# Moving rows of five transfers between DMA engines: K loads and dk stores cut into two transfers by rows

## The chip, the cores and the metric

The kernel runs on one core of one Trainium2 chip. The time is the device time of that core in microseconds (us), median of several executions. A core has 16 DMA engines, which carry every load and every store.

## The reference, cut to what matters

```python
B, H, Sq, Sk, D = 2, 32, 1, 8192, 128          # bf16
scores = einsum("bhqd,bhkd->bhqk", q, k) * D ** -0.5
out    = einsum("bhqk,bhkd->bhqd", softmax(scores), v)
# returned: out and the gradients dq, dk, dv for a given grad_out
```

There are 64 heads with one query row each. For every head 2 MB of K and 2 MB of V are read and 2 MB each of dk and dv are written, 537 MB in all. Nothing is read or written twice.

## The kernel before

K and V of a head are loaded as tiles of 128 rows (SBUF partitions) by 16 KB. There are 12 such tiles. dk and dv are computed in place of K and V and stored from the same tile, so a load has to wait until the store of the tile that it replaces has landed.

```python
load_eng = nc.sync          # SP: descriptors made by hardware
store_eng = nc.gpsimd       # POOL: descriptors made by software
...
def load(i, w, pieces=(NCH,)):                      # w: 0 for K, 1 for V
    t = kvp.tile([P, NT, D], BF16, tag=f"kv{slot_of(i, w)}", name="kvt")
    src = (v_v if w else k_v)[i]
    c = 0
    for m in pieces:
        n0, n1 = c * CH, (c + m) * CH
        pin(load_eng.dma_start(out=t[:, n0:n1, :], in_=src[:, n0:n1, :]))
        c += m
...
def outer(i, w, c, ends):                           # dk or dv, in place, then its store
    ...
    pin(store_eng.dma_start(out=dst[:, b0:b1, :], in_=h.tile[w][:, b0:b1, :]))
```

Of the kernel before, what the change touches and what calls it, by code (L numbers as in the profile page):

```python
# [16 lines left out]
CW = 64  # L17
NG = 2
NTILE = 12

@with_exitstack
def kernel(
# [12 lines left out]
    B, H, Sq, D = q.shape  # L36
# [5 lines left out]
    NT = Sk // P  # L42
# [5 lines left out]
    load_eng = nc.sync  # L48
    store_eng = nc.gpsimd
    pin = tc.keep_in_program_order  # L50
# [25 lines left out]
    def slot_of(i, w):  # L76

        n = 2 * i + w
        return n if n < NTILE else slot_of(i - NTILE // 2, 1 - w)

    def load(i, w, pieces=(NCH,)):
        h = heads[i]
        t = kvp.tile([P, NT, D], BF16, tag=f"kv{slot_of(i, w)}", name="kvt")
        h.tile[w] = t
        src = (v_v if w else k_v)[i]
        c = 0
        for m in pieces:
            n0, n1 = c * CH, (c + m) * CH
            pin(load_eng.dma_start(out=t[:, n0:n1, :], in_=src[:, n0:n1, :]))  # L89
            c += m  # L90

    load(0, 0, (1, 1, 2))

    qd_nat = evp.tile([P, CH, P], BF16, tag="ev", name="qd_nat")
    for w, a in enumerate((q, grad_out)):
        pin(load_eng.dma_start(out=qd_nat[:BH, w, :], in_=a.rearrange("b h s d -> (b h s) d")))  # L96

    load(0, 1)
    for j in range(1, min(NTILE // 2, BH)):
        load(j, 0)  # L100
        load(j, 1)
# [268 lines left out]
    def outer(i, w, c, ends):  # L370

        h = heads[i]
        n0 = c * CH
        shape = [P, CH, D // 2, 2]
        pin(
            nc.vector.tensor_tensor(  # L376
                out=h.tile[w][:, n0 : n0 + CH, :].rearrange("p n (e t) -> p n e t", t=2),
                in0=h.qb[w][:]
                .rearrange("p (e t) -> p e t", t=2)
                .unsqueeze(1)  # L380
                .to_broadcast(shape),
                in1=h.pair[w][:, n0 : n0 + CH, :].unsqueeze(2).to_broadcast(shape),
                op=ALU.mult,
            )
        )
        if c + 1 in ends:
            at = ends.index(c + 1)
            b0, b1 = (ends[at - 1] if at else 0) * CH, (c + 1) * CH
            dst = (dv_v if w else dk_v)[i]
            pin(store_eng.dma_start(out=dst[:, b0:b1, :], in_=h.tile[w][:, b0:b1, :]))  # L390

    A1 = NCH + 4
# [4 lines left out]
    last = list(range(1, NCH + 1))  # L397
    AHEAD = NTILE // 2

    prev = None  # L400
    for g in range(SL * BH + O0 + NCH + 4 - SL):
# [15 lines left out]
        if x := within(O1):  # L417
            outer(x[0], 1, x[1], last if x[0] == BH - 1 else whole)
        if x := within(O0):
            outer(x[0], 0, x[1], last if x[0] == BH - 1 else whole)  # L420
        ev = None
        if g < SL * BH:
            i, r = divmod(g, SL)
# [74 lines left out]
```

## Time and profile before

| | before |
|---|---|
| time, median of 2 runs | 1305.32 us (1304.26 to 1306.38) |
| busy: PE, DVE, ACT, POOL | 89%, 72%, 75%, 6% |
| HBM traffic over the span | 412 GB/s |
| packets of 16 KB, usual duration | 611 ns |

The prediction shows the DMA rows of the page, the load queue's waits, the end of the chain and five windows. One more part of the page is of use later, the DMA issues (out<-in, queue, operation, count, KB each, median us from issue to landing of the last share):

```profile
out_dram<-kvt POOLq DMA_DIRECT2D x126, 2048.0 KB, 40.4
kvt<-in_v_dram SPq DMA_DIRECT2D x64, 2048.0 KB, 49.3
kvt<-in_k_dram SPq DMA_DIRECT2D x63, 2048.0 KB, 49.4
```

A share is 8 packets of 611 ns. That a transfer needs eight to ten times as long is queueing: several stores and loads stand before it on the engine that finishes last.

### The profile page before, as it was taken

The numbers are of one execution on the slowest core, as the hardware profiler recorded it, in microseconds if no ns is written. First come the engines' busy times: TensorE is split into PE (matmuls) and PEld (weight loads), VectorE is DVE, ScalarE is ACT, GpSimd is POOL, SyncE is SP. The second block draws the span as 40 slices with busy tenths as digits, with TensorE's granted clock in tenths as the row PEclk, the third lists the DMA queues.
The fourth block names the chain that finished last, engine by engine and source line by source line (L and its number), as shares of the span: only waits on it lengthen the run. The fifth ranks groups of instructions, "written<-read, shape, count | busy, mean of one in ns | idle before, by whom it ended". The sixth has DMA issues, their size and how long they took to land.

```text
span 1303.1 us, 42566 instructions
## 1 busy us (share of the span) xinstructions
PE 1154.0 (89%) x19268; PEld 873.0 (67%) x19268; DVE 937.5 (72%) x2122; ACT 974.8 (75%) x641; POOL 72.4 (6%) x142
## 2 busy tenths in 40 slices
PE   6999998889898888988989888989898898888984
PEld 5777776667676666666766666667676676666662
DVE  2888887677776777767777677676776767777776
ACT  6888887777787777777778777777777777777771
POOL 0000000000000000000000000000000000000001
PEclk9999999899898999989989999898898989999986
DMA  9999999999999999999999999999999999999965
GB/s 390 423 427 427 427 427 427 428 426 430 427 427 427 427 427 429 427 428 427 429 427 427 429 427 424 418 420 425 421 416 420 419 421 421 418 421 422 394 281 206
DMA packets 38517, 539.67 MB, mean 414 GB/s; under 512 B 4544, under 2 KB 4544, under 8 KB 5824
## 3 DMA queue, kind: packets, MB, share of 16 engines
q1 hardware_dynamic: 19040, 268.51, 48.9%
q0 software_dynamic: 19296, 268.44, 48.7%
q8 instruction: 150, 2.46, 0.7%
q14 instruction: 31, 0.25, 0.0%
HBM read 268.47 MB, written 268.47 MB: 412 GB/s over the span
## 4 chain that ended last, share of the span: by engine, by line
issue 80%; DMA 11%; POOL 4%; DVE 2%; PE 1%; POOLq 0%; SPq 0%; DVEq 0%
DMA kvt<-in_v_dram 8%; POOL out_dram L390 4%; DMA out_dram<-kvt 3%; DVE kvt L376 1%; PE tp L166 1%; POOLq L390 0%; PE acc L321 0%; DVE sel L344 0%; PE dpw L177 0%; SPq L89 0%; SPq L96 0%; DVE sel L338 0%; PE sw L177 0%; PE acc L358 0%; DVE pair L252 0%
## 5 line engine op out<-in xcount | busy, mean ns | idle before, releaser
L168 ACT COPY ev<-tp 128x2048 bf16<-128x2048 bf16 x512 | 954.0, 1865 | 300.3 <-PE tp L166 290.6
L166 PE MATMUL tp<-ident_bf,kvt 128*128 128x128 bf16 x8192 | 573.4, 226 | 108.9 <-DMA kvt<-in_v_dram 91.1
L376 DVE TENSOR_TENSOR kvt<-qb,pair 128x2048 bf16<-128x2048 bf16 x512 | 621.1, 1214 | 0.2
L166 PEld LDWEIGHTS <-kvt 128*128 128x128 bf16 x8192 | 501.4, 102 | 116.2 <-DMA kvt<-in_v_dram 95.8
L177 PEld LDWEIGHTS <-ev 128*128 128x128 bf16 x8192 | 242.8, 96 | 211.2 <-issue 164.4
L321 PE MATMUL acc<-kvt,dS_pad 128*64 128x512 bf16 x1024 | 177.2, 430 | 1.3 <-DVE dqT L361 1.3
L321 PE MATMUL acc<-kvt,E_pad 128*64 128x512 bf16 x1024 | 159.8, 392 | 0.0
L177 PE MATMUL dpw<-qdT,ev 128*128 128x1 bf16 x4096 | 140.9, 164 | 12.0 <-DVE qb L159 10.7
L189 DVE TENSOR_REDUCE mp<-sw 128x1 f32<-128x64 f32 x64 | 14.3, 224 | 186.5 <-PE sw L177 186.5
L344 DVE SCALAR_TENSOR_TENSOR sel<-acc,diag,sel 128x128 f32<-128x128 f32 x384 | 134.6, 351 | 13.6
L177 PE MATMUL sw<-qdT,ev 128*128 128x1 bf16 x4096 | 142.5, 164 | 1.1 <-ACT ev L168 1.1
L390 POOL DMA_DIRECT2D out_dram<-kvt x134 | 71.3, 532 | 1219.2 <-DVE kvt L376 1186.8
L321 PEld LDWEIGHTS <-dS_pad 128*64 128x64 bf16 x1024 | 38.5, 113 | 26.9 <-issue 9.4
L229 DVE CAST E_pad<-E_f 128x64 bf16<-128x64 f32 x64 | 12.5, 195 | 60.6 <-ACT E_f L220 60.6
L321 PEld LDWEIGHTS <-E_pad 128*64 128x64 bf16 x1024 | 36.3, 108 | 21.0 <-issue 0.2
L358 PE MATMUL acc<-ones,sel 128*128 128x1 f32 x256 | 43.3, 239 | 6.2 <-DVE sel L344 6.2
L264 PE MATMUL dpw<-ld,ones 128*128 128x1 f32 x256 | 46.3, 250 | 0.1
L338 DVE TENSOR_SCALAR sel<-acc,diag 128x128 f32<-128x128 f32 x128 | 44.0, 344 | 0.0
L358 PEld LDWEIGHTS acc<-ones,sel 128*128 128x128 f32 x256 | 39.0, 193 | 7.3 <-DVE sel L344 7.3
L235 DVE CUSTOM_DVE_ANT_0 junk<-E_f,dpw 128x64 bf16<-128x64 f32 x64 | 14.1, 220 | 40.2 <-PE dpw L177 40.2
L159 DVE CAST qb<-dpw 128x128 bf16<-128x128 f32 x128 | 35.4, 277 | 6.0 <-PE dpw L150 6.0
L264 PEld LDWEIGHTS dpw<-ld,ones 128*128 128x128 f32 x256 | 38.2, 188 | 0.5 <-DVE ld L235 0.5
(42 smaller groups left out, 303.2 us busy)
## 6 DMA issues: line engine op xcount, KB each, us to landing
out_dram<-kvt POOLq DMA_DIRECT2D x126, 2048.0 KB, 40.4
kvt<-in_v_dram SPq DMA_DIRECT2D x64, 2048.0 KB, 49.3
kvt<-in_k_dram SPq DMA_DIRECT2D x63, 2048.0 KB, 49.4
out_dram<-kvt POOLq DMA_DIRECT2D x8, 512.0 KB, 11.3
kvt<-in_k_dram SPq DMA_DIRECT2D x2, 512.0 KB, 4.5
kvt<-in_k_dram SPq DMA_DIRECT2D x1, 1024.0 KB, 7.1
out_dram<-nat SPq DMA_DIRECT2D x2, 16.0 KB, 5.0
qd_nat<-in_q_dram SPq DMA_DIRECT2D x1, 16.0 KB, 6.8
```

The costliest lines, as they stand in the source:

```text
L159: pin(nc.vector.tensor_copy(out=h.qb[w][:], in_=h.qbp))
L166: pin(nc.tensor.transpose(tp[:, t, :], src[:, c * CH + t, :], ident_bf[:]))
L168: pin(nc.scalar.copy(out=ev[:], in_=tp[:]))
L177: nc.tensor.matmul(dst[:, c * CH + t : c * CH + t + 1], lhsT=ev[:, t, :], rhs=qdT[:, w, i : i + 1], start=True, stop=True,)
L189: pin(nc.vector.reduce_max(out=h.mp[:], in_=h.s, axis=AX.X))
L264: nc.tensor.matmul(out, lhsT=ones[:].to_broadcast([P, P]), rhs=col, start=True, stop=True)
L321: nc.tensor.matmul(h.acc[w][g : g + CW, :], lhsT=wts[:, n0 : n0 + CW], rhs=rows[:, n0 : n0 + QT, :].rearrange("p n d -> p (n d)"), start=( ...
L338: nc.vector.tensor_scalar(out=h.sel[:], in0=block, scalar1=diag[:, 0:1], scalar2=None, op0=ALU.mult)
L344: nc.vector.scalar_tensor_tensor(out=h.sel[:], in0=block, scalar=diag[:, b : b + 1], in1=h.sel[:], op0=ALU.mult, op1=ALU.add,)
L358: nc.tensor.matmul(h.acc[w][:, 0:1], lhsT=h.sel[:], rhs=ones[:], start=True, stop=True)
L376: nc.vector.tensor_tensor(out=h.tile[w][:, n0 : n0 + CH, :].rearrange("p n (e t) -> p n e t", t=2), in0=h.qb[w][:] .rearrange("p (e t) -> ...
L390: pin(store_eng.dma_start(out=dst[:, b0:b1, :], in_=h.tile[w][:, b0:b1, :]))
```

## The change

The intent is to even out the load of the DMA engines. Transfers of a row count that 16 doesn't divide use fewer engines, so three K loads and two dk stores are each cut into two transfers by rows, such that four to seven engines take most of the 2 MB and the others get relief.

```diff
+HEADS_IN = {10: (119, 9), 16: (102, 26), 22: (76, 52)}
+HEADS_OUT = {26: (119, 9), 32: (9, 119)}
...
+    def by_rows(eng, dst, src, rows):
+        p = 0
+        for m in rows:
+            pin(
+                eng.dma_start(out=dst[p : p + m], in_=src[p : p + m], max_dma_last_dim=NT * D)
+            )
+            p += m
...
+        if w == 0 and i in HEADS_IN:
+            by_rows(load_eng, t, src, HEADS_IN[i])
+            return
...
+            if w == 0 and i in HEADS_OUT:
+                pin(store_eng.inc_swdge_sem([], [], mode="reset_dge_cursor"))
+                by_rows(store_eng, dst, h.tile[w], HEADS_OUT[i])
+                return
```

The `max_dma_last_dim` makes two packets of 8 KB out of each row of 16 KB. The reset puts the cursor of the stores, the engine at which the next store that doesn't take all 16 begins, back to engine 0 (the prediction has the rule).

## The prediction

> **What bounds the kernel now.** The page first: no compute engine is near its limit (PE 89% busy, of modelled ends; DVE 72%, ACT 75%), while the DMA row is full for 38 of the 40 slices and the rate flat.
>
> ```profile
> DMA  9999999999999999999999999999999999999965
> GB/s 390 423 427 427 427 427 427 428 426 430 427 427 427 427 427 429 427 428 427 429 427 427 429 427 424 418 420 425 421 416 420 419 421 421 418 421 422 394 281 206
> q1 hardware_dynamic: 19040, 268.51, 48.9%
> q0 software_dynamic: 19296, 268.44, 48.7%
> q8 instruction: 150, 2.46, 0.7%
> ```
>
> The last line is the fetching of instructions, a third user of the same 16 engines. The rate is 427 in the first half and near 420 from slice 25 on: something gets worse. Next, who waits for whom on the load queue, and the chain of waits near the end:
>
> ```profile
> SPq L89 <- DMA out_dram<-kvt: 1140.6, 116, 24.2
> ...
> 1154.90 49.14 DMA kvt<-in_v_dram
> ...
> 1215.54 49.35 DMA kvt<-in_v_dram
> 1264.90 0.05 issue
> 1264.94 1.49 PE tp L166 x16
> ```
>
> Almost every load is issued only when a store has landed and freed its tile; a load then needs 49 us to land. A transfer puts 8 rows of 16 KB on each engine, and a packet of that size took 611 ns, so 8 rows beside 8 of a store (the queues alternate) are about 9.8 us of work. The other 40 us are queue, but not on all engines. The trace holds the 16 completion times of each transfer, one for each DMA engine, without the engine's number. Sorted, for the last V load (issued at 1215.5 us): seven from 1225.2 to 1226.4, eight from 1238.9 to 1243.0, one at 1264.9. So there are seven fast engines, eight middle ones, and one straggler, 22 us behind all others. The lag grows: behind the first engine the straggler was 4.4 us late for the load issued at 9.6 us, 12.5 at 252.5, 21.8 at 496.1, 27.4 at 617.5. Then it stays near 39 to 40, because the fast engines have caught up with the issue (10 to 12 us from issue to landing there, their own work and nothing else) and cannot get further ahead: that is the fall from 427 to 421. The windows (columns: busy time with count of PE, PEld, DVE, ACT, POOL; clock; DMA share; GB/s) show both this and the drain:
>
> ```profile
> 100.00:700.00 600.00, 544.18 (x9110) 412.01 (x9109) 442.42 (x997) 460.80 (x303) 32.41 (x61) 0.95 1.01 428
> 750.00:1200.00 450.00, 399.94 (x6688) 302.54 (x6686) 325.32 (x738) 338.06 (x223) 23.39 (x44) 0.95 1.01 421
> ...
> 1226.00:1243.00 17.00, 16.80 (x288) 12.40 (x285) 13.37 (x33) 14.22 (x10) 0.53 (x1) 0.95 0.86 363
> 1243.00:1265.00 22.00, 18.66 (x306) 14.05 (x303) 15.79 (x35) 16.23 (x11) 1.44 (x3) 0.92 0.54 226
> 1265.00:1292.00 27.00, 19.30 (x209) 11.81 (x209) 21.66 (x45) 7.77 (x6) 4.77 (x10) 0.70 0.72 289
> ```
>
> From 1226 us engines run dry while the straggler still owes loads. The end is its end too: the last quarter store is issued at 1291.6, 15 engines finish it by 1295.1, the straggler at 1301.1. **The straggler bounds the kernel from the first stores to the last byte.** Its pace: loads are issued 101.1 us per ten late in the run (1023.4 to 1124.5), 10.11 us for 16 of its packets, 0.632 us each; a fast one has 0.607 (the next packet starts some 4 ns before the 611 are over).
>
> **What the Trainium skill says.** *DMA: Bandwidth & Descriptors*, section "Why a DMA increments its semaphore by 16 and not by 1": the number of engines k is the largest up to 16 that divides the slowest dimension of both sides; loads from SP use the lowest-numbered k engines, stores from GpSimd k consecutive ones from a round-robin cursor, though some such direct copies take 16 engines all the same. Before, every transfer has a row count divisible by 16 and 16 completions, which agrees; smaller k does not occur. The same page, "Latency and other measured facts": engines 7 and 15 are usually slower than the rest. One straggler is seen here, its number is not. *Runtime: NRT & Kernel Launch*, "Instruction fetch mechanics": instructions come in blocks of 16 KiB over DMA; the 150 packets on q8 agree, and their durations repeat roughly every eight packets, which fits eight engines doing the fetching: the middle group.
>
> **The change part by part.** No arithmetic moves; on GpSimd, two cursor resets and two more stores are added, on SP three more loads. All that counts is rows per engine. With the skill's rule, 119 = 7 x 17 goes to 7 engines, 9 to 9, 102 = 6 x 17 to 6, 76 = 4 x 19 to 4, 26 and 52 to 13. Rows per engine, against 8 in an even transfer:
>
> ```
> engines       0-3   4-5    6    7-8   9-12  13-15
> K load 10      18    18   18      1     0      0
> K load 16      19    19    2      2     2      0
> K load 22      23     4    4      4     4      0
> dk store 26    17    17   17      1     1      1
> dk store 32     1     1    1      1    17     17
> sum            78    59   42      9    24     18
> less 5 x 8    +38   +19   +2    -31   -16    -22
> ```
>
> The store splits, which start from cursor 0, relieve exactly 7 and 8 of the two row sets; the loads relieve all above 6. This is a design against a straggler numbered 7, eight middle engines 8 to 15, and fast ones 0 to 6: 7 + 8 + 1, as the completion times have it. That the numbers belong to the groups so is my choice; the trace does not show it, and the skill's engine 7 supports it.
>
> Natural arrival at the last V load, if no engine had to wait: straggler 1264.9 and middle about 1241 as measured; fast: the lag of 4.1 us per 100 us (27.4 us at 667 us, where the load issued at 617.5 lands last) gives 52 at 1265, so 1213. Add rows:
>
> Engines 0 to 3: 1213 + 38 x 0.607 = 1236. Engines 4 and 5: 1213 + 19 x 0.607 = 1225. Engine 6: 1214. Engine 7: 1264.9 - 31 x 0.632 = 1245.3. Engine 8: 1241 - 19 = 1222. Engines 9 to 12: 1241 - 10 = 1231. Engines 13 to 15: 1241 - 13 = 1228.
>
> Engine 7 remains last, by 9 us. So the gain is 31 x 0.632 = 19.6 us, no more: the moved load comes out of an engine's work that is on the path everywhere, and lands on engines that had 52 us to spare. The tail shifts with it: after the last V load the straggler has stores until 1301.1, 36.2 us, and the compute up to the last store 26.7 us plus 3.5 to land; both stay. 1305.3 - 19.6 = 1285.7.
>
> Costs: K tiles 10, 16 and 22 land later. Engines 0 to 3 get 15 extra rows in the worst load, 18 us with stores between. All three put 36 rows (22 us) more on them and 17 (11 us) less on engine 7; at 400 us their natural lead is 16, so they are then about 17 us behind it. A load's slack is the 39 us of queue, so nothing should run dry. The pieces of 8 KB cost 0.306 against 0.3035 for half a large packet (such packets took 309 ns, 3 ns of overlap), under 0.2 us in all. A GpSimd reset falls in an engine 6% busy.
>
> **The rivals.** (1) The stores take 16 engines, the skill's exception: then only the loads relieve engine 7, 17 rows, 10.7 us: 1294.6. For it: no store of before shows k below 16; against: the odd row counts and the resets only make sense if k follows. (2) The straggler is 15 and the middle group 0 to 7. Then engine 15 gains 22 rows, 13.9 us, but engines 0 to 3 go from 1241 to 1264: the end barely moves, 1300 to 1308. For it: the skill names 15 as well; against: the author's choice of rows, which would be senseless. (3) Port conflicts: *DMA: Bandwidth & Descriptors*, "The descriptor swizzle", has each engine write one SBUF port in a 128-partition transfer; 17 or 19 rows on one engine cross several, so several engines may meet at one port. Only the row transfers are concerned, and ports average half load each way since loads and stores are equal; estimated at a few us on engines 0 to 6, within their margin of 9: 1286 to 1291. (4) A reset or the wider skew makes GpSimd or the loads wait for an emptied queue, up to a transfer's 40 us each: 1295 to 1330. Nothing in the profile speaks for it. (5) Over 2% faster would need 1279.2, 26 us; engine 7 loses only 19.6.
>
> **Range and chances.** I give the sum 75%, rivals 1 and 3 together 15, 2 and 4 five each. The predicted time is 1286 us, range 1281 to 1300; faster by over 2% 0.05, within 2% 0.92, slower by over 2% 0.03.
>
> **What would show it.** Right: the straggler's last V load completes near 1245, the slowest of the others about 9 us before, not 22; the drain from full DMA to the last load shrinks from 39 to about 30 us; the rate stays near 427 in slices 25 to 36; small row transfers show few completions late and the rest at once. Stores 26 and 32 in which one engine's share is 17 rows decide rival 1; K load 22 landing past its queue of 49 us by more than 20 speaks for 3. Wrong: a straggler of the same 22 us (then it is not engine 7 or 8), or new idle in the DMA row near 110 to 400 or 560 to 700 us (rival 4).

## The result, and the profile after

| | before | after |
|---|---|---|
| time, median of 2 runs | 1305.32 us | 1324.78 us (1324.24 to 1325.33) |
| ratio | | 1.0149, 95% interval 1.0105 to 1.0193 |
| HBM traffic over the span | 412 GB/s | 406 GB/s |

A ratio is the mean time of one kernel's fast runs over that of the other's of the same rounds, so it is not quite the ratio of the medians in the table. The change is 19.5 us slower; a gain of 19.6 us was predicted, and the range ended at 1300. That it stayed within 2%, which the prediction had given 0.92, is luck: the sign was wrong. All its outputs were correct.

The DMA part of the page of the changed kernel:

```profile
DMA  9999999999999999999999999999999999999973
GB/s 390 424 427 426 427 412 427 428 420 375 398 396 408 421 408 417 425 420 373 422 417 414 423 425 427 426 429 423 426 425 423 424 425 423 420 425 423 421 312 135
q1 hardware_dynamic: 19428, 268.51, 48.6%
q0 software_dynamic: 20224, 268.45, 48.4%
q8 instruction: 150, 2.46, 0.7%
```

The rate, flat at 427 in this part of the run before, has holes now: slice 6 (412), slices 10 to 16 (375 to 421) and slice 19 (373). A slice is 33 us, and K loads 10, 16 and 22 are issued at 130, 250 and 389 us, the cut stores at 573 and 678 us. And the last slice is at 135 GB/s where it was 206.

The windows of the changed kernel (columns as in the prediction) show what was going on in the holes and at the end:

```profile
170.00:210.00 40.00, 16.03 (x262) 11.96 (x259) 12.24 (x28) 13.11 (x10) 1.07 (x2) 0.70 1.01 416
...
290.00:330.00 40.00, 26.77 (x446) 20.09 (x444) 21.92 (x50) 23.01 (x16) 1.60 (x3) 0.88 1.01 383
330.00:470.00 140.00, 110.06 (x1862) 83.95 (x1862) 89.64 (x205) 93.68 (x62) 6.39 (x12) 0.87 0.99 407
```

```profile
1243.00:1271.00 28.00, 24.64 (x412) 18.47 (x409) 21.83 (x49) 21.60 (x14) 1.64 (x4) 0.94 0.94 395
1271.00:1300.00 29.00, 18.28 (x210) 11.59 (x210) 22.30 (x48) 7.77 (x6) 3.53 (x7) 0.76 0.65 265
1300.00:1323.40 23.40, 0.00 (x0) 0.00 (x0) 0.00 (x0) 0.00 (x0) 1.60 (x3) 0.50 0.22 88
```

Between 170 and 210 us the PE worked 16 of 40 us (35.7 before): it stood waiting for K tile 10, of which the seven engines delivered their shares only 63 to 71 us after the issue. The DMA share is still 1.01, because loads were queued on every engine. Between 290 and 330 us the DMA share is again 1.01, but with only 383 GB/s: the packets took longer. In the last 23 us no compute engine does anything; one engine empties its queue. The completion times of the last store of the changed kernel, after its issue at 1311.8 us: 15 of them at 2.7 to 2.9 us, one at 9.3. It was worse for the quarter store issued at 1297.0: 15 at 2.8 to 2.9 us, one at 20.4. So there is still one straggler, and its end has moved from 1301.1 to 1321.1 us. In the loads it hardly shows any more: the last V load landed at 1271.1 us on its last engine and at 1266.6 on the one before (1264.9 and 1243.0 in the kernel before).

Who waited for whom on the store queue of the changed kernel (us in total, times, longest), and the issues, show a side effect:

```profile
POOL out_dram L407 <- DVE kvt L389: 1089.4, 116, 32.4
POOL out_dram L407 <- DMA out_dram<-kvt: 61.8, 9, 12.9
```

```profile
out_dram<-kvt POOLq DMA_DIRECT2D x124, 2048.0 KB, 56.8
kvt<-in_v_dram SPq DMA_DIRECT2D x64, 2048.0 KB, 35.1
kvt<-in_k_dram SPq DMA_DIRECT2D x60, 2048.0 KB, 32.7
```

The backlog moved from the load queue (where the straggler's lag stood before) to the store queue: loads land after 33 to 35 us in place of 49, stores after 57 in place of 40. The last quarter stores were issued 4.7 to 5.1 us apart, each held until an earlier store had landed on the straggler; that is the second of the two waits. It doesn't lengthen the straggler's own work.

### The profile page after: what moved, and what is told of

Its sections match the earlier page's. It is cut to its first block, busy times and chain, and to the rows that moved or that the text cites. A ratio compares the mean times of both kernels' runs of the same rounds, so it can differ in the third digit from the quotient of the medians.

```text
span 1323.4 us, 42579 instructions
## 1 busy us (share of the span) xinstructions
PE 1133.0 (86%) x19268; PEld 861.5 (65%) x19268; DVE 936.4 (71%) x2122; ACT 975.3 (74%) x641; POOL 74.8 (6%) x144
## 4 chain that ended last, share of the span: by engine, by line
issue 34%; PE 22%; another core or an unknown queue 20%; DMA 13%; DVE 6%; POOL 2%; ACT 1%; SPq 0%; POOLq 0%
PE tp L179 10%; DMA kvt<-in_v_dram 8%; PE acc L334 6%; DMA out_dram<-kvt 4%; DVE kvt L389 4%; PE sw L190 3%; PE dpw L190 3%; POOL out_dram L407 2%; DVE sel L357 1%; ACT ev L181 1%; DMA kvt<-in_k_dram 1%; PE dpw L277 1%; DMA qd_nat<-in_q_dram 1%; DVE sel L351 0%
## 5 line engine op out<-in xcount | busy, mean ns | idle before, releaser
L179 PE MATMUL tp<-ident_bf,kvt 128*128 128x128 bf16 x8192 | 562.9, 224 | 127.6 <-DMA kvt<-in_k_dram 74.4
L179 PEld LDWEIGHTS <-kvt 128*128 128x128 bf16 x8192 | 494.2, 101 | 132.8 <-issue 61.8
L334 PE MATMUL acc<-kvt,dS_pad 128*64 128x512 bf16 x1024 | 168.6, 411 | 4.0 <-issue 2.1
```

The costliest lines, as they stand in the source:

```text
L179: pin(nc.tensor.transpose(tp[:, t, :], src[:, c * CH + t, :], ident_bf[:]))
L334: nc.tensor.matmul(h.acc[w][g : g + CW, :], lhsT=wts[:, n0 : n0 + CW], rhs=rows[:, n0 : n0 + QT, :].rearrange("p n d -> p (n d)"), start=( ...
```

## The experiments

Theory A: the straggler is not engine 7. It is among the engines that the row loads burden, and the time is the rows on it. Its rivals: B, the straggler is engine 7, it was relieved as planned, and late tiles and stalls cost more than that gave; and, after the first runs, C: a transfer cut by rows costs every engine time beyond its rows. Under C there are again two: D, the rows are on other engines than usual and those get into each other's way; E, the small packets or the number of transfers cost the time. Twelve kernels ran in four groups; the kernel before had a median of 1305.05, 1304.54, 1304.59 and 1306.88 us in them.

### Which number has the straggler

**x1_probe** (one look, state unknown). The kernel before, with tiny loads of 1 to 16 rows behind every fourth big load:

```diff
+        n = 2 * i + w - 60
+        if n >= 0 and n % 4 == 0 and n // 4 < 16:
+            m = n // 4 + 1
+            pin(load_eng.dma_start(out=probe[0:m, m - 1], in_=q_rows[0:m, 0:32]))
```

> The kernel before, with a tiny load of 1, 2, ... 16 rows queued right behind every fourth big load from the 60th load on. A load of m rows with m up to 16 should run on the m lowest-numbered engines, so its m completions stand right behind those of the big load before it and give each engine's number. Theory A (the straggler is one of engines 0 to 3, so the row loads burdened it): the late completion, 22 to 39 us behind the middle ones, is there in every probe of 4 or more rows. Theory B (the straggler is engine 7 as predicted, and the time went into stalls): it is there from the probe of 8 rows on, and not in those of 1 to 7. The time should stay within 5 us of the kernel before.

Measured: 1311.12 us, 6 us over the kernel before, a little more than the 5 expected. The idea is that a load of m rows runs on engines 0 to m - 1 (the rule for k that the prediction cites), so each further probe adds one engine to those that answer. Behind the big load, in the same queue, its completions are about 1 us after that engine's share of the big load. Sorted, in us (F: with the fast group of the big load, M: with the middle one, S: with the straggler):

```
rows  completions                                                     new engine
  4   F 678.7 679.7 683.2 686.6                                       0 to 3: F
  5   F 716.4 716.8 721.5 727.3                           S 748.5     4: S
  6   F 753.2 753.4 758.5 767.4    M 772.7                S 790.7     5: M
  7   F 791.9 792.5 795.2 804.9    M 811.7 813.6          S 832.4     6: M
  8   F 829.4 829.7 829.8 832.7 841.1  M 853.1 853.7      S 874.3     7: F
```

The straggler's completion appears with the fifth row: it is **engine 4**. Going on to 16 rows, engine 8 comes in with the fast ones, 9 to 14 with the middle ones and 15 with the fast ones. So the groups are 0 to 3, 7, 8, 15 (fast), 5, 6, 9 to 14 (middle) and 4. The prediction had the sizes of the groups right and the numbers wrong. Engine 7 is a fast one.

**a1_probe** (one look, state unknown). The same in the changed kernel, four probes of 4 and 5 rows:

```diff
+        if w == 1 and i in (42, 46, 50, 54):
+            at = (i - 42) // 4
+            m = (4, 5)[at % 2]
+            pin(load_eng.dma_start(out=probe[0:m, at], in_=q_rows[0:m, 0:32]))
```

> The changed kernel with four probes of 4, 5, 4 and 5 rows behind V loads 42, 46, 50 and 54, as in x1_probe. There one engine ends each load about 20 us after its issue, the others after 11 to 16. If the engine that ends the changed kernel is number 4, the probes of 5 rows have a completion behind that last one and those of 4 rows do not. If it is one of 0 to 3, which the loads burdened most, the probes of 4 rows have it too. If it is 7, none has. Time within 5 us of the changed kernel's 1325.

Measured: 1324.3 us. The probe of 4 rows behind V load 50: 1000.2 to 1000.6, while that load ended at 1006.1 on its last engine. The probe of 5 rows behind V load 54: 1081.2 to 1082.3 and one at 1088.3, right behind that load's last share at 1087.2. The engine that ends the changed kernel is number 4 as well.

With this the table of the prediction is to be read anew: engine 4 gets 18 + 19 + 4 rows in the loads in place of 24, and 17 + 1 in the stores in place of 16. That is 19 rows more, not 31 less, or 19 x 0.632 = 12.0 us.

### Loads alone, stores alone

**x2_loads** (3 rounds):

```diff
-HEADS_OUT = {26: (119, 9), 32: (9, 119)}
+HEADS_OUT = {}
```

> The change with the three row loads alone, the two stores whole again. Theory A (straggler in 0 to 3): it gets 18+19+23 rows in place of 24, 36 more, times 0.632 us = 22.8 us: 1322 to 1330. Theory B (straggler 7, stalls in the row loads): it gets 17 rows less but the stalls of slices 9 to 16 stay; between 1300 and 1315.

**x3_stores** (3 rounds):

```diff
-HEADS_IN = {10: (119, 9), 16: (102, 26), 22: (76, 52)}
+HEADS_IN = {}
```

> The change with the two row stores alone, the three loads whole again. Theory A: a straggler in 0 to 3 gets 17+1 rows in place of 16, so +1 us: 1303 to 1310. Theory B: the straggler 7 gets 1+1 rows in place of 16, 14 rows less, 8.8 us: 1293 to 1299.

Measured: x2_loads 1324.72 us, ratio 1.0147 (1.0132 to 1.0162); x3_stores 1307.13 us, ratio 1.0012 (0.9995 to 1.0029). The loads make the whole loss, the stores nothing that is sure. The expectations were written for any straggler from 0 to 3; that x2_loads lies in theory A's 1322 to 1330 is luck, for it was reckoned with 36 rows. For engine 4 the loads add 17 rows, 10.7 us, and the stores 2 rows, 1.3 us. The stores agree. The loads cost 19.7 us: 9.0 us, or 3.0 a load, are not explained by rows.

### Large packets

**x4_16k** (3 rounds):

```diff
-eng.dma_start(out=dst[p : p + m], in_=src[p : p + m], max_dma_last_dim=NT * D)
+eng.dma_start(out=dst[p : p + m], in_=src[p : p + m])
```

> The change with whole rows of 16 KB as packets in place of two of 8 KB. In the changed kernel K load 10 reached its seven engines 63 to 71 us after issue, which fits 34 small packets that each wait for one 16 KB store packet (34 x 0.913 = 31 us behind the tile before); with 17 large packets it should be 17 x 1.21 = 21 us behind, so 53 to 61 us. Theory A (the total is set by rows on the straggler): the time stays at 1320 to 1328. Theory B (stalls from late tiles): most of the shortfall comes back, 1295 to 1312.

Measured: 1334.41 us, ratio 1.0233 (1.0209 to 1.0256). K load 10 reached its seven engines after 54.7 to 64.0 us, as expected within 3 us, against 63.2 to 71.3 in the changed kernel. So the late tile has the expected reason: the two queues take turns packet by packet, and a packet of 8 KB that alternates with 16 KB of a store gets a third of the engine, not half. But the tile came earlier (the PE worked 24 of the 40 us from 170 on, in place of 16) and the kernel was slower still. Late tiles are not what the end hangs on. Theory B falls here, and theory A as I had put it was also too good: the time rose above its 1328, 10 us over the changed kernel with the same rows on every engine.

### Relief for engine 4, and for engine 7

**z2_skip4** and **z3_skip7** (3 rounds each), loads whole:

```diff
-HEADS_IN = {10: (119, 9), 16: (102, 26), 22: (76, 52)}
-HEADS_OUT = {26: (119, 9), 32: (9, 119)}
+HEADS_IN = {}
+HEADS_OUT = {h: (5, 120, 3) for h in (8, 16, 24, 32, 40, 48)}   # z2_skip4
+HEADS_OUT = {h: (8, 120) for h in (8, 16, 24, 32, 40, 48)}      # z3_skip7
```

> The kernel before with six dk stores (heads 8 to 48) cut into 5, 120 and 3 rows from cursor 0. By k = 5, 15 and 3 this leaves engine 4, the straggler of the probes, 2 rows in place of 8 and gives 1 more to engines 0 to 3, 5 and 6. Theory A (the end is the rows on engine 4): 36 rows less, 22.8 us, of which 22 count before the middle engines bind: 1281 to 1287. Theory B (engine 4 is not the cause, or the stores are not numbered as the loads are): 1303 to 1312.

> The same six stores cut into 8 and 120 rows, which leaves engine 7 one row in place of eight and engine 4 nine. Theory A (straggler 4): 6 rows more on it, 3.8 us: 1307 to 1312. Theory of the prediction (straggler 7): 42 rows less, 26.5 us, of which 22 count: 1282 to 1288.

Measured: z2_skip4 1289.56 us, ratio 0.9877 (0.9858 to 0.9897); z3_skip7 1312.83 us, ratio 1.0062 (1.0047 to 1.0077). Relief of engine 4 makes the kernel 15 us faster and relief of engine 7 makes it 8 us slower: the straggler's number is the cause of the sign. Both are just outside the ranges of theory A (1281 to 1287, 1307 to 1312), behind what rows alone give. z3_skip7 should have lost 3.8 and lost 8.3; the difference, 4.5 us for six cut stores, makes 0.75 us for each. z2_skip4 should have gained 22 by its expectation and gained 15, but these 7 us are not all the cost of cuts. Its last store landed on 14 engines by 1281.8 us and on two at 1285.9 and 1287.5: the end is no longer one engine's. These two are probably the middle engines 5 and 6, to which the cuts gave 6 rows each (3.6 us); if they are the latest of the middle ones, the most that rows could give is 22 - 3.6, about 18 us (an estimate), and some 3 us are left for the six cuts.

The drain of z2_skip4 in windows (columns as before):

```profile
1226.00:1242.00 16.00, 13.00 (x227) 9.93 (x225) 12.02 (x28) 11.69 (x9) 1.06 (x2) 1.00 0.94 400
1242.00:1268.00 26.00, 18.10 (x205) 10.94 (x202) 21.78 (x46) 7.77 (x6) 3.20 (x6) 0.72 0.87 365
```

The last V load lands at 1241.5 us in place of 1264.9, and after it the engines still work at 365 GB/s: where before one engine alone owed stores, here ten do (of the store issued at 1241.2 us, six engines had landed their shares by 1248.8, ten from 1259.4 to 1272.5). z2_skip4 is the fastest kernel and beats both.

### What a cut costs beyond the rows

**z5_four** (3 rounds): the three loads in a cut that takes 4 rows each from engine 4.

```diff
+HEADS_IN = {h: (76, 52) for h in (10, 16, 22)}
+HEADS_OUT = {}
```

> The three loads of the change, each cut into 76 and 52 rows, so that engine 4 gets 4 rows in place of 8 each time and engines 0 to 3 get 23. Theory A, rows alone: 12 rows less on engine 4, 7.6 us: 1296 to 1300. Theory C (a row load costs every engine time beyond its rows; the change's loads alone cost 19.7 us where 17 rows make 10.7, so about 3 us a load): 1304 to 1312.

**z1_even** (3 rounds): twelve loads in a cut that gives every engine its 8 rows.

```diff
+HEADS_IN = {h: (112, 16) for h in range(10, 46, 3)}
+HEADS_OUT = {}
```

> Twelve K loads (heads 10 to 43) cut into 112 and 16 rows, k = 16 both times: every engine keeps 8 rows, only the order of rows on the engines and the packets of 8 KB are as in the change. Theory C1 (the cutting itself costs about 3 us a load): 1330 to 1345. Theory C2 (the extra comes from the unevenness: one tile's 16 shares landing far apart): 1303 to 1310.

Measured: z5_four 1305.97 us, ratio 1.0010 (0.9995 to 1.0025): the 7.6 us of relief are eaten, 9.0 us for three loads, 3.0 each, the same as in x2_loads. z1_even 1349.25 us, ratio 1.0333 (1.0303 to 1.0363): 44.7 us for twelve loads, 3.7 each, with no engine burdened; that is above C1's 1345 and far above C2's 1310. Cutting a load by rows costs by itself; C1 holds. Here is the rate of z1_even, with a hole in most places where a cut load stands:

```profile
GB/s 390 422 427 427 425 421 423 422 389 419 399 428 385 412 400 405 418 375 422 374 423 378 421 376 412 379 422 421 426 422 422 420 418 424 417 420 421 357 214 257
```

**c1_cols** (3 rounds): the same twelve loads, but cut by columns.

```diff
+        if w == 0 and i in range(10, 46, 3):
+            pieces = (NCH // 2, NCH // 2)
```

> The same twelve K loads as in z1_even, again in two transfers each and in packets of 8 KB, but cut by columns: both transfers have all 128 rows, so each engine keeps its usual rows. Theory D (rows out of their usual place: several engines meet at one port of SBUF, packets stretch): the 44 us of z1_even are gone, 1303 to 1309, and packets over 1.5 times their usual length are as rare as before (about 160 on the load queue against 1098 in z1_even). Theory E (small packets beside 16 KB store packets, or one more transfer a tile, cost the time): 1340 to 1352 again.

**z7_even16k** (3 rounds): z1_even with the one-line edit of x4_16k.

> z1_even with rows of 16 KB in one packet. Theory D: an engine stays on one wrong port twice as long at a time but the rows are the same, so about as slow as z1_even, 1340 to 1362. Theory E: near the kernel before, 1303 to 1312.

Measured: c1_cols 1311.76 us, ratio 1.0053 (1.0037 to 1.0068); z7_even16k 1344.59 us, ratio 1.0304 (1.0287 to 1.0321). By columns, 0.6 us a load are left of 3.7, with the same number of transfers and the same packet size (a little above theory D's 1309); by rows, large packets cost nearly as much as small ones, 3.3 us a load (in x4_16k, 17 us over the rows for three cut loads and two cut stores, they cost more). Theory E falls, and the rows are the reason. The packet records suggest in which way. Of each packet over its usual duration (611 ns, or 309 for 8 KB) I take what is over, sum it over the run, take off the 244 us that the kernel before has, and divide by 16 engines:

| kernel | 8 KB packets of cut loads over 1.5 times the usual | us stretched per engine, over before | time lost, less the rows on engine 4 |
|---|---|---|---|
| z1_even | 512 of 3200 | 38 | 45 |
| z7_even16k | cut loads in 16 KB | 40 | 40 |
| x4_16k | cut loads in 16 KB | 24 | 17 |
| x2_loads | 40 of 896 | 14 | 9 |
| changed kernel | 43 of 896 | 12 | 7.5 |
| z5_four | 26 of 896 | 5 | 9 |
| c1_cols | 4 of 3200 | 1 | 7 |
| z3_skip7 | no cut load | 5 | 4.5 |
| z2_skip4 | no cut load | -1.5 | 7 (see above) |

For z1_even this is 234 + 181 + 443 us (store packets, load packets of 8 KB and of 16 KB), 858 in all, less 244, over 16: 38. The stretch follows the loss roughly, within 7 us in the kernels with cut loads. So packets of rows that are not with their usual engine take longer, and those of other loads beside them too (586 of the large load packets of z1_even were over 1.5 times the usual, 161 before).

That they meet at the ports of SBUF is argued, not shown: the Trainium skill, *DMA: Bandwidth & Descriptors*, "The descriptor swizzle", has each engine write the partitions of one port in a transfer of 128 partitions, and with 112 or 119 rows the shares cannot lie so. No record names a port or an engine, and the rows of a cut load lie elsewhere in HBM for each engine, too; no run separates the two. The 0.6 us a load that a cut by columns costs are not explained.

### A finer balance that failed

**z4_mix** (3 rounds), z2_skip4 with three more cut stores:

```diff
+HEADS_OUT = {**{h: (5, 120, 3) for h in (8, 16, 24, 32, 40, 48)}, **{h: (15, 95, 18) for h in (20, 36, 52)}}
```

> The six stores of z2_skip4 and three more (heads 20, 36, 52) cut into 15, 95 and 18 rows, which take 5 rows each from engine 4, 5 to 7 from the middle engines, and give 11 to 12 to engines 15 and 0 to 3. Rows alone: engine 4 loses 51 rows, 32 us, engines 0 to 3 gain 42 and end last, 26 us before the straggler of before: 1279. With 0.7 to 1.1 us for each cut store, as z3_skip7 and z2_skip4 show: 1285 to 1290. If the cuts cost more than they give: above the 1290 of z2_skip4.

Measured: 1312.22 us, ratio 1.0061 (1.0046 to 1.0076), 23 us slower than z2_skip4 though it should have gained a little on it. At the end of z4_mix one engine alone is late again, 20 us. In the third of these stores the piece of 95 rows has five late completions, 42.8 to 55.2 and 82.5 us after issue, and the last of them comes 21.7 us after the last of the 15-row piece before it (1145.3 after 1123.6), far too long for 3 rows (5.5 us at 1.83 a row, stores and loads in turn): the straggler seems to be one of the five engines with 19 rows. That would be so if the piece of 15 rows had left the cursor at 0 and the 95 rows had gone to engines 0 to 4. Then engine 4 has 20 rows in place of 8 three times, 36 more, and the six other stores take 36 off: 0 in sum, and nine cuts at the 0.75 us of z3_skip7 make 6.8 us, where 7.6 were measured. It fits, but I did not test it. What the cursor does after 15 rows stays open.

## Why the prediction was wrong

**The bound was right.** In the kernel before, in the changed one and in z3_skip7 the end is one engine's work; in z2_skip4 it passed on to two others. Rows taken off engine 4 or put on it moved the end in that direction (z2_skip4, z3_skip7, the changed kernel), and once the cost of the cuts is counted the 0.632 us a row account for the sizes to within some 3 us. Why engine 4 is the slow one stays open. It has as many rows as the others, but its packets are longer: from 1252.6 to 1257.5 us, where in the kernel before it alone still has loads and stores to do, its eight packets of 16 KB took 618 to 689 ns, 644 on average, against the usual 611. In the changed kernel it had 611 again for each of four packets from 1305 us on, when no compute ran.

**The step that failed** is this one: "This is a design against a straggler numbered 7, eight middle engines 8 to 15, and fast ones 0 to 6 ... That the numbers belong to the groups so is my choice; the trace does not show it, and the skill's engine 7 supports it." I read the numbers off the change's intention and off a general remark on engines 7 and 15. The runs: the straggler is 4, in both kernels; 7 and 15 are fast. Its term of the sum was -31 rows, -19.6 us; it is +19 rows, +12.0 us. The sign that the prediction named for being right did not come: the straggler's last V load was to land near 1245 us and landed at 1271.1. Rival 2 (the straggler is another than 7, "1300 to 1308") was of the right kind, but it had been worked out for engine 15 alone and given too little weight.

**Which engines a transfer takes** was right for the loads: the completions of the six row transfers were 7, 9, 6, 13, 4 and 13, as the divisors say, and the lowest-numbered ones answer. Of the stores, the 119 rows of dk store 26 show nine completions at 9.8 to 13.1 us after issue and seven at 35.2 to 50.4 (15.5 to 20.7 and 23.9 to 29.8 in the whole store before it), so seven engines took them and rival 1 did not come to pass; z2_skip4 and z3_skip7 fit the cursor as well. z4_mix is the exception.

**The stretch of the row transfers**, rival 3, was named, placed on "engines 0 to 6, within their margin" and sized "a few us". It comes to 9.0 us for the three loads (what rows leave over in x2_loads, and the same again in z5_four with another cut). It counts in full, so it must fall on the straggler, too, which has no margin; this is inferred, for the packets carry no engine's number. 12.0 + 9.0 is 21; measured were 19.5 us, so the terms are right to 2 us. The sign that the prediction gave for this rival was seen, but decides nothing: K load 22 had its last share 74.5 us after issue, 25 past the queue's 49, and 23 rows at 1.83 us (next paragraph) in place of 8 at 1.21 make 32 us more without any stretch.

**The landing of the cut loads** was mis-sized: a row with stores between was taken as 1.21 us; in two packets of 8 KB, each beside a store packet of 0.607, it is 2 x 0.913 = 1.83 us, which its cost of "under 0.2 us in all" for the small packets left out. This stopped the PE (the window from 170 us on), but x4_16k shows that the end does not hang on it.

**A reading that the trace does not bear out**, though nothing in the sum hangs on it: the durations of the 150 instruction packets do not repeat "roughly every eight packets". In the kernel before, they correlate at -0.09 with those eight packets earlier and at 0.56 with those 16 earlier (1 would be an exact repeat, 0 none). So the middle group is not explained. (The size would fit: 150 packets of 0.99 us over eight engines are 18 us each, an estimate.)

**Rival 4** was wrong in its cause: the two resets took 18 ns each. The holes in the rate where it expected them are of stretched packets and of fast engines short of work: of the V load issued at 340.1 us, nine engines had landed their shares after 7.2 to 9.5 us, which leaves no queue, and the last after 56.1.

## What to carry to other kernels

Where one DMA engine sets the end, find its number by measurement before rows are moved: a tiny load of m rows behind a big one, for m = 1, 2, 3 and so on, names it in one run. A transfer that leaves the slow engine out is then worth its rows, until other engines end the kernel; but cut a large load by columns if it has to be cut at all, for each cut by rows cost 3.0 to 3.7 us here (over 5 in x4_16k), one by columns 0.6, and a cut store about 0.75 or less.

## What the Trainium skill lacked or had wrong

- *DMA: Bandwidth & Descriptors*, "Latency and other measured facts", has engines 7 and 15 as usually slower. In these runs it was engine 4 (in the numbering in which a load of m rows takes 0 to m - 1), 22 us behind all others at the end; 7 and 15 were among the seven fastest. In the changed kernel it was 4 as well. The record has these runs on three chips: x1_probe on 2, a1_probe on 7, z2_skip4 and z3_skip7 on 13.
- The same page, "Why a DMA increments its semaphore by 16 and not by 1": its rule for k held for all loads (7, 9, 6, 13, 4, 13 completions). For stores with a cursor it fits the changed kernel, z2_skip4 and z3_skip7, but seems not to for the stores with a piece of 15 rows in z4_mix (1312 us where 1285 to 1290 were expected from it).
- The same page, "The descriptor swizzle", tells where the rows of a 128-row transfer go, and no page has what it costs in full queues to leave that order: 3.0 to 3.7 us for each 2 MB load cut by rows (over 5 in x4_16k), 0.6 us for one cut by columns.
- The same page, "Queues, rings and completion order", has queues taking turns packet by packet, and the runs agree: from 1252.6 to 1257.5 us in the kernel before, where one engine works alone, loads and stores alternate with every record of the trace, a row of 16 KB or a 4-byte record. They show a consequence that the page does not draw: 17 rows in packets of 8 KB reached their engines 63 to 71 us after issue, in packets of 16 KB 55 to 64.
- *Runtime: NRT & Kernel Launch*, "Instruction fetch mechanics", does not say on which engines instructions are fetched. Eight engines were 12 to 18 us behind the seven fast ones at the last V load of the kernel before; by the probes these are 5, 6 and 9 to 14. That the fetching makes the difference is not shown.
